# Two batches interleaved: batch 0 begins with six column tiles of the MLP, and three changeovers between batches 0 and 1 instead of five

## The chip, the cores and the metric

The kernel runs on one core of one Trainium2 chip. The metric is the device time of one execution in microseconds (us), the median of several runs. A profile of one execution shows what each engine did: TensorE (PE, with its weight loads as PEld), VectorE (DVE), ScalarE (ACT), GpSimd (POOL), and the queue SP, which here only issues DMAs. All times inside the execution count from the first instruction.

## The reference

An attention between 512 tokens and 32 state rows, in both directions, for 8 batches of 8 heads, and behind it one MLP with squared ReLU over all 4,608 rows:

```python
B, H, S, Ns, D = (8, 8, 512, 32, 64)
scores = scale * x @ state.T ;  a = softmax(scores);   xread = a @ state
scores2 = scale * state @ x.T;  a2 = softmax(scores2); sread = a2 @ x
rows = concatenate([xread, sread])            # 512 + 32 rows for each batch, 8 heads x 64 = 512 columns
out = relu(rows @ w_in) ** 2 @ w_out          # 512 -> 2048 -> 512
```

The weights `w_in` and `w_out` arrive as 64-bit floats and are brought to 32 bits on the chip.

## The kernel before

**Arithmetic.** Each large matmul is done as three: every float is split into a rounded high part and a rest (`split`: a cast on ACT at L97, a subtraction on DVE or POOL at L98), and hi x hi, lo x hi and hi x lo are summed.

**State first.** The kernel never forms `xread`. For the tokens it multiplies the state with `w_in` once (`z_part`: `L192` for the first six pieces, `L204` for the others), writes the result `zd` to DRAM and reads back what a batch needs (`z_fetch`, `L230`). The first matmul of the MLP is then attention weights times z.

**A unit.** The MLP works on one batch (512 tokens) and one column tile of 128 of the 2,048 hidden columns at a time, 16 column tiles (`NFC`) for each batch. I call this a unit, and number the units from 1 as they are worked through. In `mlp`, `up` issues 6 matmuls (L394) into `ph`; ACT takes the ReLU (L396); the square is ACT's for the first ten units (L398) and DVE's from then on (L400); ACT casts to `g_hi` (L97), and DVE closes the unit with `g_lo` (L98). `down` then issues 12 matmuls (L420) into four accumulators `po`, one for each 128 tokens. `down` runs two units behind `up`.

**Parts and changeovers.** `BOTH` (L67) cuts the column tiles of batches 0 and 1 into parts that alternate: an entry (b, c) means that batch b goes on to column tile c. At the end of a part `rows` empties the four accumulators into `sums[b]`: in a batch's first part by two copies on DVE (L441) and two on ACT (L439), in later parts by four adds on DVE (L601). Behind (0, NFC) and (1, NFC) the batches 2 to 7 follow whole, and at the end the same MLP runs once for the 256 state rows.

**Weights.** Each column tile needs two conversions on DVE. For `w_in`: a load into `w_raw` (L159), an absolute value on ACT (L107), then four DVE steps (L108, L109, L113, L117) that give `wf`; `wf` goes to DRAM (`wd`) and, from the seventh piece on, is split into `w` (L97, L98). For `w_out`: a load into `wo_raw` (L446), the same five steps to `wof`, and a split into `wo_hi` and `wo_lo` (POOL at L98). The raw words share `RAW` = 4 buffers, `wf` and `wof` have two each.

**Attention.** For batches 0 and 1 the scores run as plain matmuls (`pst`, L301) behind a scaling of the state (L248), then two softmaxes (L306 to L342). From batch 2 on they run as split matmuls (L291, with `sp_hl` from L251 and L252). The attention's weights `a_hi`, `a_lo` must be there before the batch's first unit. Two loads of x for each batch (L267) and two for the way back (L273) go through SP.

**What sets the order.** The class `Ahead` holds two lists of steps, `weights` and `reads` (the attention and its way back), each group with a due time in slots (two a unit): for weights twice the unit at which a column tile is first used (`at`, L466), for the attention of batch b twice the unit at which b begins, less one (`begins`, L567). `aux`, called twice a unit, issues as many steps as the due times ask for. Behind that, a scheduler moves instructions on each engine by its own estimate of their times; the engines then run them in the order printed in the section on the change.

Of the kernel before, what the change touches and what calls it, by code (L numbers as in the profile page):

```python
# [18 lines left out]
def memory_attention_then_relu2_ffn(  # L19
# [33 lines left out]
    NFC = DF // P  # L53
# [10 lines left out]
    XRAW = 2  # L64
    PLAIN_Z = 6
    PLAIN_X = 2
    BOTH = ((0, 2), (1, 6), (0, 10), (1, 10), (0, NFC), (1, NFC))  # L67
    LATE = 3

    def pool_early(early):  # L70
# [385 lines left out]
    parts, upto = [], [0] * B  # L456
    for b, c in BOTH + tuple((b, NFC) for b in range(2, B)):
        parts.append((b, range(upto[b], c)))
# [217 lines left out]
```

## Time and profile before

| what | value |
|---|---|
| median of 3 runs | 734.75 us (734.13 to 735.08) |
| the profiled execution | 734.07 us, of which 732.2 us are its span |
| granted TensorE clock, mean | 0.963 |
| HBM read and written | 60.03 MB and 29.88 MB |
| the chain that ended last | PE 74%, DMA 11%, DVE 8%, ACT 3% |

The page gives busy times and shares for each engine; a busy share is a mean over stages that have different limits. Its second part cuts the span into 40 slices of 18.3 us, with the busy share of each engine in tenths. A view by stretches gives busy time in any stretch, the granted TensorE clock (1.00 is full speed) and the share of time that the 16 DMA engines were busy. The timeline has one row for each instruction or run of like instructions: start, duration, engine, line, output and inputs, and in brackets the idle time ahead of it and what ended it. Durations overlap, since an engine begins an instruction before the one ahead has ended; the distance of two starts is what an instruction costs in a row of like ones.

### The profile page before, as it was taken

How to read it: one execution, taken by the hardware profiler on the slowest of the kernel's cores; microseconds unless marked ns; L12 is line 12 of the kernel's file. 1: busy time of each engine (PE TensorE's matmuls, PEld its weight loads, DVE VectorE, ACT ScalarE, POOL GpSimd, SP SyncE). 2: the span in 40 equal slices, each digit the busy share in tenths (PEclk: the TensorE clock that was granted, in tenths of full speed). 3: DMA queues.
4: the chain of work that ended last, by engine and by line, in shares of the span. 5: the costliest groups of instructions: out<-in, count | busy, mean ns of one | idle time of the engine just before them, and what ended most of it. 6: DMA issues, size and time to landing. Idle time of an engine off the chain costs nothing.

```text
span 732.2 us, 9312 instructions
## 1 busy us (share of the span) xinstructions
PE 679.1 (93%) x3152; PEld 554.3 (76%) x3152; DVE 476.6 (65%) x797; ACT 392.7 (54%) x711; POOL 197.6 (27%) x181
## 2 busy tenths in 40 slices
PE   4865898889999899999999999999999999999994
PEld 1434677768888788888888878878888888888893
DVE  5889798798956944356954694797755445443541
ACT  2656477566766664357654554656554345332441
POOL 2334121146662540025402322343152022000000
PEclk9677799999999999999999999999999999999998
DMA  9757877684464641143433211422141012100410
GB/s 265 252 175 249 243 244 235 201 221 133 133 213 129 195 127 59 47 140 119 136 108 116 86 59 58 143 87 86 60 144 58 31 33 82 42 1 9 135 59 30
DMA packets 72435, 90.52 MB, mean 124 GB/s; under 512 B 3780, under 2 KB 55748, under 8 KB 72388
## 3 DMA queue, kind: packets, MB, share of 16 engines
q1 hardware_dynamic: 54980, 73.15, 32.2%
q10 hardware_dynamic: 17408, 16.78, 6.8%
q8 instruction: 25, 0.41, 0.3%
q14 instruction: 22, 0.18, 0.1%
HBM read 60.03 MB, written 29.88 MB: 123 GB/s over the span
## 4 chain that ended last, share of the span: by engine, by line
PE 74%; DMA 11%; DVE 8%; ACT 3%; issue 2%; SPq 0%; POOL 0%; ACTq 0%; DVEq 0%
PE po L420 43%; PE ph L394 23%; DMA wo_raw<-w_out 3%; DMA z_raw<-zd 3%; PE pr L357 2%; PE pz L204 2%; DMA xn_raw<-xn 2%; DMA st_f<-stT 1%; PE pq L291 1%; DMA zd<-z_stage 1%; DVE sp_hl L252 1%; PE pz L192 1%; DVE wof L113 1%; DVE wof L117 1%; PE pt L345 1%
## 5 line engine op out<-in xcount | busy, mean ns | idle before, releaser
L420 PE MATMUL po<-wo_hi,g_hi 128*128 128x512 f32 x544 | 219.1, 405 | 15.5 <-ACT g_hi L97 12.1
L420 PE MATMUL po<-wo_lo,g_hi 128*128 128x512 f32 x544 | 216.4, 399 | 0.0
L400 DVE TENSOR_TENSOR ph<-ph,r 128x512 f32<-128x512 f32 (+1 forms) x134 | 89.0, 664 | 152.0 <-ACT r L396 151.9
L396 ACT ACTIVATE r<-ph 128x512 f32<-128x512 f32 (+1 forms) x144 | 82.6, 574 | 168.1 <-PE ph L394 167.4
L420 PE MATMUL po<-wo_hi,g_lo 128*128 128x512 f32 x544 | 152.4, 392 | 0.4
L420 PEld LDWEIGHTS po<-wo_hi,g_hi 128*128 128x128 f32 x544 | 103.9, 191 | 39.9 <-ACT g_hi L97 14.7
L420 PEld LDWEIGHTS po<-wo_lo,g_hi 128*128 128x128 f32 x544 | 104.9, 193 | 20.3 <-issue 0.7
L420 PEld LDWEIGHTS po<-wo_hi,g_lo 128*128 128x128 f32 x544 | 101.3, 189 | 22.0 <-DVE g_lo L98 1.6
L98 DVE TENSOR_TENSOR g_lo<-ph,g_hi 128x512 fp32r<-128x512 f32 (+1 forms) x144 | 94.5, 656 | 34.2 <-ACT g_hi L97 24.6
L97 ACT CAST g_hi<-ph 128x512 fp32r<-128x512 f32 (+1 forms) x144 | 81.1, 563 | 43.0 <-DVE ph L400 37.8
L394 PE MATMUL ph<-a_hi,z_hi 128*128 128x512 f32 x256 | 81.4, 399 | 0.6 <-DVE g_lo L98 0.6
L394 PE MATMUL ph<-a_hi,z_lo 128*128 128x512 f32 x256 | 79.7, 393 | 0.0
L394 PE MATMUL ph<-a_lo,z_hi 128*128 128x512 f32 x256 | 79.3, 391 | 0.0
L98 POOL TENSOR_TENSOR xn_hl<-xn_raw,xn_hl 128x1024 fp32r<-128x1024 f32 x16 | 39.2, 2449 | 147.9 <-ACT xn_hl L97 79.6
L183 POOL TENSOR_TENSOR w<-wf,w 64x512 fp32r<-64x512 f32 x32 | 43.5, 1360 | 59.6 <-ACT w L182 52.5
L394 PEld LDWEIGHTS ph<-a_hi,z_lo 128*128 128x128 f32 x256 | 48.4, 189 | 11.0 <-DVE z_lo L98 0.3
L394 PEld LDWEIGHTS ph<-a_hi,z_hi 128*128 128x128 f32 x256 | 47.8, 193 | 11.5 <-DVE g_lo L98 1.3
L394 PEld LDWEIGHTS ph<-a_lo,z_hi 128*128 128x128 f32 x256 | 48.2, 189 | 10.3
L98 DVE TENSOR_TENSOR z_lo<-z_raw,z_hi 128x512 fp32r<-128x512 f32 x64 | 50.2, 784 | 4.3 <-ACT z_hi L97 4.3
L97 ACT CAST z_hi<-z_raw 128x512 fp32r<-128x512 f32 x64 | 39.4, 615 | 12.3 <-DMA z_raw<-zd 11.9
L98 POOL TENSOR_TENSOR xt_hl<-xt_raw,xt_hl 128x1024 fp32r<-128x1024 f32 x12 | 29.3, 2438 | 58.5 <-ACT xt_hl L97 36.0
L98 POOL TENSOR_TENSOR wo_lo<-wof,wo_hi 128x512 fp32r<-128x512 f32 x16 | 22.5, 1407 | 79.4 <-ACT wo_hi L97 79.4
(98 smaller groups left out, 854.4 us busy)
## 6 DMA issues: line engine op xcount, KB each, us to landing
zd<-z_stage ACTq DMA_DIRECT2D x64, 256.0 KB
z_raw<-zd SPq DMA_DIRECT2D x63, 256.0 KB
xt_raw<-xT SPq DMA_DIRECT2D x16, 512.0 KB
w_raw<-w_in SPq DMA_DIRECT2D x16, 512.0 KB
wo_raw<-w_out SPq DMA_DIRECT2D x16, 512.0 KB
xn_raw<-xn SPq DMA_DIRECT2D x16, 512.0 KB
out<-sum SPq DMA_DIRECT2D x32, 256.0 KB
wd<-wf SPq DMA_DIRECT2D x16, 256.0 KB
```

The source lines that it names most:

```text
L97: nc.scalar.copy(out=hi, in_=src)
L98: eng_lo.tensor_sub(out=lo, in0=src, in1=hi.bitcast(F32))
L113: nc.vector.scalar_tensor_tensor(out=bits, in0=high, scalar=-0x40000000, in1=bits, op0=ALU.bitwise_and, op1=ALU.bitwise_or,)
L117: nc.vector.scalar_tensor_tensor(out=bits, in0=low, scalar=29, in1=bits, op0=ALU.logical_shift_right, op1=ALU.bitwise_or,)
L183: nc.gpsimd.tensor_sub(out=w[other], in0=wf[own], in1=w[own].bitcast(F32))
L192: nc.tensor.matmul(pz[:, q, :], lhsT=st["raw"][own, h, :], rhs=box["wf"][own, q, :], start=True, stop=True,)
L204: nc.tensor.matmul(pz[:, q, :], lhsT=a[:, h, :], rhs=w, start=j == 0, stop=j == len(todo) - 1,)
L357: nc.tensor.matmul(pr[:, q].rearrange("p i c -> p (i c)"), lhsT=my["e"][:, t, q].rearrange("p i n -> p (i n)"), rhs=my["xn"][:, t, q].rear ...
L394: nc.tensor.matmul(ph, lhsT=w, rhs=v, start=i == 0, stop=i == len(todo) - 1)
L396: nc.scalar.activation(r, ph, AF.Relu)
L400: nc.vector.tensor_mul(out=ph, in0=ph, in1=r)
L420: nc.tensor.matmul(po[t], lhsT=g, rhs=w, start=i == 0 and j == 0, stop=i == last and j == 2)
```

## The change

```diff
-    BOTH = ((0, 2), (1, 6), (0, 10), (1, 10), (0, NFC), (1, NFC))
+    BOTH = ((0, 6), (1, 10), (0, NFC), (1, NFC))
```

The 32 units of batches 0 and 1 run in this order, as ranges of column tiles:

| | units 1-2 | 3-6 | 7-8 | 9-16 | 17-20 | 21-26 | 27-32 |
|---|---|---|---|---|---|---|---|
| before | batch 0: 0-1 | batch 1: 0-3 | batch 1: 4-5 | batch 0: 2-9 | batch 1: 6-9 | batch 0: 10-15 | batch 1: 10-15 |
| now | batch 0: 0-1 | batch 0: 2-5 | batch 1: 0-1 | batch 1: 2-9 | batch 0: 6-9 | batch 0: 10-15 | batch 1: 10-15 |

Column tiles 2 to 5 are first used at units 3 to 6 instead of 5 to 8, tiles 6 to 15 at the same units as before. Batch 1 begins at unit 7 instead of unit 3, so its attention falls due four units later. Changeovers between the two batches stand ahead of units 7, 17 and 27 instead of 3, 9, 17, 21 and 27. Eight of the sixteen adds of L601 fall away: each batch has two parts instead of three. Nothing else is removed or added; the numbers of matmuls, loads and conversions stay the same.

How the instructions move shows in the printed order of each engine. Counted on DVE, the instructions ahead of and with a unit's closing `g_lo`:

| closing step of unit | 3 | 5 | 7 | 9 | 13 | 15 | 17 | 24 |
|---|---|---|---|---|---|---|---|---|
| before | 108 | 126 | 143 | 160 | 193 | 212 | 229 | 282 |
| now | 97 | 132 | 160 | 175 | 206 | 219 | 226 | 273 |

At the three places below, the rows are DVE's (`wf`: w_in's conversion, `wof`: w_out's, `w_1`: the low part of a split piece of w_in, `g_lo`: a unit's closing step). The first place is the way from the sixth to the seventh closing step. Before, the whole of it:

```order
L98 TENSOR_TENSOR g_lo<-ph,g_hi 128x512
L113 SCALAR_TENSOR_TENSOR wof<-wo_raw,wof 128x512
L117 SCALAR_TENSOR_TENSOR wf<-w_raw,wf 128x512
L117 SCALAR_TENSOR_TENSOR wof<-wo_raw,wof 128x512
L108 TENSOR_SCALAR wof<-wof 128x512
L109 TENSOR_SCALAR wof<-wof 128x512
L98 TENSOR_TENSOR w_1_741<-wf,w_0_740 128x512
L113 SCALAR_TENSOR_TENSOR wof<-wo_raw,wof 128x512
L98 TENSOR_TENSOR g_lo<-ph,g_hi 128x512
```

Now, its last eleven of 27 rows:

```order
L109 TENSOR_SCALAR wf<-wf 128x512
L108 TENSOR_SCALAR wof<-wof 128x512
L113 SCALAR_TENSOR_TENSOR wf<-w_raw,wf 128x512
L98 TENSOR_TENSOR w_1_871<-wf,w_0_870 128x512
L109 TENSOR_SCALAR wof<-wof 128x512
L117 SCALAR_TENSOR_TENSOR wf<-w_raw,wf 128x512
L98 TENSOR_TENSOR z_lo<-z_raw,z_hi 128x512
L113 SCALAR_TENSOR_TENSOR wof<-wo_raw,wof 128x512
L117 SCALAR_TENSOR_TENSOR wof<-wo_raw,wof 128x512
L98 TENSOR_TENSOR w_1_990<-wf,w_0_989 128x512
L98 TENSOR_TENSOR g_lo<-ph,g_hi 128x512
```

Seven instructions stood between the two closing steps; now 25 do, the last transposition of batch 1's attention and two copies of accumulators among the rows not shown. On PE the products of state and w_in that run as L204 stand further ahead in return: 72 of them, instead of 35, come before the seventh unit's first L420.

The second place is the end of the weights' conversions. Before, it lies behind the sixteenth closing step (the first row here), and the adds are those of the changeover ahead of unit 17:

```order
L98 TENSOR_TENSOR g_lo<-ph,g_hi 128x512
L108 TENSOR_SCALAR wof<-wof 128x512
L109 TENSOR_SCALAR wof<-wof 128x512
L113 SCALAR_TENSOR_TENSOR wof<-wo_raw,wof 128x512
L117 SCALAR_TENSOR_TENSOR wof<-wo_raw,wof 128x512
L400 TENSOR_TENSOR ph<-ph,r 128x512
L601 TENSOR_TENSOR sum<-sum,po_950 128x512
L601 TENSOR_TENSOR sum<-sum,po_951 128x512
L601 TENSOR_TENSOR sum<-sum,po_952 128x512
L98 TENSOR_TENSOR g_lo<-ph,g_hi 128x512
```

Now it lies ahead of the fifteenth closing step (the fifth row here; the eighth is the sixteenth):

```order
L109 TENSOR_SCALAR wof<-wof 128x512
L113 SCALAR_TENSOR_TENSOR wof<-wo_raw,wof 128x512
L117 SCALAR_TENSOR_TENSOR wof<-wo_raw,wof 128x512
L400 TENSOR_TENSOR ph<-ph,r 128x512
L98 TENSOR_TENSOR g_lo<-ph,g_hi 128x512
L400 TENSOR_TENSOR ph<-ph,r 128x512
L98 TENSOR_TENSOR z_lo<-z_raw,z_hi 128x512
L98 TENSOR_TENSOR g_lo<-ph,g_hi 128x512
L400 TENSOR_TENSOR ph<-ph,r 128x512
L441 COPY sum<-po_874 128x512
L441 COPY sum<-po_876 128x512
```

The last conversion has moved from the changeover to a place two units ahead of it, and two copies stand where three adds stood.

The third place is the changeover from batch 1 to batch 2, ahead of unit 33. Before (`st`, `sp_hl`, `q` and `at` belong to the attention of later batches):

```order
L297 TENSOR_TENSOR st<-pq,st_low 64x512
L251 TENSOR_SCALAR sp_hl<-sp_raw 64x4x32
L329 STREAM_TRANSPOSE at<-q_2322 128x512
L251 TENSOR_SCALAR sp_hl<-sp_raw 64x4x32
L400 TENSOR_TENSOR ph<-ph,r 128x512
L252 SCALAR_TENSOR_TENSOR sp_hl<-sp_raw,sp_hl 64x4x32
L297 TENSOR_TENSOR st<-pq,st_low 64x512
L252 SCALAR_TENSOR_TENSOR sp_hl<-sp_raw,sp_hl 64x4x32
L601 TENSOR_TENSOR sum<-sum,po_1760 128x512
L601 TENSOR_TENSOR sum<-sum,po_1761 128x512
L601 TENSOR_TENSOR sum<-sum,po_1762 128x512
```

Now:

```order
L297 TENSOR_TENSOR st<-pq,st_low 64x512
L400 TENSOR_TENSOR ph<-ph,r 128x512
L601 TENSOR_TENSOR sum<-sum,po_1744 128x512
L601 TENSOR_TENSOR sum<-sum,po_1745 128x512
L98 TENSOR_TENSOR g_lo<-ph,g_hi 128x512
L601 TENSOR_TENSOR sum<-sum,po_1746 128x512
L601 TENSOR_TENSOR sum<-sum,po_1747 128x512
L400 TENSOR_TENSOR ph<-ph,r 128x512
```

The writing of `sp_hl` and the transposition have moved behind the adds.

On SP, the two loads of batch 2's x move from behind the sixth and seventh load of w_in to behind the ninth and eleventh.

## The prediction

> **What bounds the kernel now.** I read the page first: which engine is full, and when.
>
> ```profile
> PE 679.1 (93%) x3152; PEld 554.3 (76%) x3152; DVE 476.6 (65%) x797; ACT 392.7 (54%) x711; POOL 197.6 (27%) x181
> PE   4865898889999899999999999999999999999994
> DVE  5889798798956944356954694797755445443541
> DMA  9757877684464641143433211422141012100410
> ```
>
> TensorE (PE) is the bound, but not from the start: its slices are full only from about the tenth on (18.3 us each). Before that VectorE (DVE) and the DMA engines have high digits. So the change, which rearranges the first 32 units, can only give or take time where PE still waits. The table by stretches sizes that (PE, PEld, DVE, ACT, POOL busy; then the granted clock, the DMA share, GB/s):
>
> ```profile
> 20.00:47.00 27.00, 19.75 (x47) 10.79 (x47) 21.70 (x47) 16.14 (x36) 8.19 (x7) 0.69 0.70 226
> 47.00:100.00 53.00, 40.97 (x165) 31.36 (x164) 46.36 (x77) 31.19 (x57) 16.38 (x12) 0.81 0.72 223
> 100.00:150.00 50.00, 44.84 (x214) 36.47 (x213) 41.86 (x70) 31.41 (x59) 9.47 (x7) 0.97 0.74 234
> 150.00:170.00 20.00, 17.12 (x75) 13.63 (x74) 18.20 (x24) 13.99 (x26) 11.56 (x8) 0.91 0.68 191
> 170.00:240.00 70.00, 70.00 (x338) 58.45 (x338) 53.38 (x93) 47.80 (x85) 36.01 (x31) 1.00 0.47 148
> 240.00:250.00 10.00, 8.14 (x41) 6.24 (x40) 9.91 (x15) 7.05 (x14) 7.39 (x5) 1.00 0.49 153
> ```
>
> From 170 to 240 us PE works 70.00 of 70 us: nothing can be won there. Time is lost in the first 170 us and once more at 240 to 250. In each lossy stretch DVE is at 80 to 99%, so DVE's queue, which runs in program order, is what to count. A unit (one column tile of one batch) is closed on DVE by the step that writes g_lo; the timeline has the first, the seventh and the fifteenth of these at:
>
> ```profile
> 46.98 0.62 DVE L98 TENSOR_TENSOR g_lo<-ph,g_hi 128x512 fp32r<-128x512 f32 x1
> 100.02 0.68 DVE L98 TENSOR_TENSOR g_lo<-ph,g_hi 128x512 fp32r<-128x512 f32 x1
> 150.61 0.68 DVE L98 TENSOR_TENSOR g_lo<-ph,g_hi 128x512 fp32r<-128x512 f32 x1
> ```
>
> **The change part by part.** PE's work is the same; only its waits and its slow-clock time differ. I follow four places and count, from the order of the instructions, what DVE has to do ahead of a closing step. Prices are the groups by line:
>
> ```profile
> L108 DVE TENSOR_SCALAR wf<-wf 128x512 f32<-128x512 f32 x16 | 8.0, 500 | 9.4 <-ACT wf L107 9.4
> L109 DVE TENSOR_SCALAR wf<-wf 128x512 int32<-128x512 int32 x16 | 7.7, 484 | 0.2
> L113 DVE SCALAR_TENSOR_TENSOR wf<-w_raw,wf 128x512 int32<-128x512 int32 x16 | 15.2, 949 | 0.1
> L117 DVE SCALAR_TENSOR_TENSOR wf<-w_raw,wf 128x512 int32<-128x512 int32 x16 | 11.9, 746 | 0.0
> L108 DVE TENSOR_SCALAR wof<-wof 128x512 f32<-128x512 f32 x16 | 9.0, 560 | 7.7 <-ACT wof L107 7.7
> L109 DVE TENSOR_SCALAR wof<-wof 128x512 int32<-128x512 int32 x16 | 8.6, 540 | 0.2
> L113 DVE SCALAR_TENSOR_TENSOR wof<-wo_raw,wof 128x512 int32<-128x512 int32 x16 | 13.3, 834 | 0.1
> L117 DVE SCALAR_TENSOR_TENSOR wof<-wo_raw,wof 128x512 int32<-128x512 int32 x16 | 14.1, 882 | 0.1
> L98 DVE TENSOR_TENSOR w<-wf,w 128x512 fp32r<-128x512 f32 x10 | 8.6, 859 | 0.2
> L98 DVE TENSOR_TENSOR z_lo<-z_raw,z_hi 128x512 fp32r<-128x512 f32 x64 | 50.2, 784 | 4.3 <-ACT z_hi L97 4.3
> ```
>
> A, up to the seventh unit (batch 1's first one now). Ahead of its closing step stand 160 DVE instructions instead of 143. More are two conversions of w_in (0.500 + 0.484 + 0.949 + 0.746 = 2.68 each, 5.4), one of w_out with a second L117 (0.560 + 0.540 + 0.834 + 2 x 0.882 = 3.7), three splits of w (2.6) and one z_lo (0.8): 12.4 us. From 47 to 100 us DVE is idle for 53 - 46.36 = 6.6 us; if all that fills up, the closing step comes 12.4 - 6.6 = 5.8 us late, if none does, 12.4. I take 8.4, nearer the lower end, since the third closing step has 11 instructions fewer ahead of it than before (batch 1's attention no longer stands there), so this stretch starts earlier. Against that, PE has by then issued 72 instead of 35 of the products of state and w_in that run as 128x256 matmuls, one each 0.12 us:
>
> ```profile
> 159.36 0.28 PE L204 MATMUL pz<-w,stz_lo 128*128 128x256 f32 x1
> 159.48 0.40 PE L204 MATMUL pz<-w,stz_hi 128*128 128x256 f32 x2
> ```
>
> 37 x 0.12 = 4.4 us of PE's work done in advance. A = +8.4 - 4.4 = **+4.0 us** (1.4 to 8.0).
>
> B, from the seventh to the fifteenth unit. At the fifteenth 219 instructions stand against 212: two w_out conversions and one split more (5.6 + 0.9), two copies of 0.68 fewer: +5.1 us. So DVE has 12.4 - 5.1 = 7.3 us less to do in this stretch, of 41.86. PE loses 50 - 44.84 = 5.2 us to idleness here and 0.03 x 50 = 1.5 to the clock, together 6.7; the gain lies between 0 (if the loads of the weights set the pace, DMA share 0.74) and 6.7. With DVE clearly below PE's load but the loads unchanged I take half: **-3.3 us**.
>
> C, units 16 to 18. Here a changeover meets the last w_out conversions:
>
> ```profile
> 156.59 0.41 DVE L108 TENSOR_SCALAR wof<-wof 128x512 f32<-128x512 f32 x1
> 157.04 1.41 DVE L109 TENSOR_SCALAR wof<-wof 128x512 int32<-128x512 int32 x1
> 158.49 1.67 DVE L113 SCALAR_TENSOR_TENSOR wof<-wo_raw,wof 128x512 int32<-128x512 int32 x1
> 160.19 1.65 DVE L117 SCALAR_TENSOR_TENSOR wof<-wo_raw,wof 128x512 int32<-128x512 int32 x1
> 161.77 0.68 DVE L400 TENSOR_TENSOR ph<-ph,r 128x512 f32<-128x512 f32 x1
> 163.18 0.77 PE L420 MATMUL po<-wo_hi,g_hi 128*128 128x512 f32 x1 [2.58 <-ACT g_hi L97]
> 163.75 0.63 PE L420 MATMUL po<-wo_lo,g_hi 128*128 128x512 f32 x1
> 164.17 0.63 PE L420 MATMUL po<-wo_hi,g_hi 128*128 128x512 f32 x1
> 168.21 0.39 PE L420 MATMUL po<-wo_hi,g_hi 128*128 128x512 f32 x1
> 168.44 0.40 PE L420 MATMUL po<-wo_lo,g_hi 128*128 128x512 f32 x1
> ```
>
> The square of unit 17 (L400) stands behind four conversion steps; PE waits 2.58 us for the cast of that square, and then starts a matmul every 0.42 us (163.75, 164.17) until it is back at 0.23 (168.21, 168.44). The stretch loses 2.88 us idle and 0.09 x 20 = 1.8 to the clock: 4.7. In the change the conversions end ahead of the fifteenth closing step; what stands ahead of the seventeenth is two copies, and three adds are gone (229 instructions against 226). The changeover itself stays. Gain 0 to 4.7; I take **-3.5 us**, near the upper end, as the blocking rows are gone.
>
> [...]
>
> D, unit 33, where batch 2 begins:
>
> ```profile
> 239.89 2.52 DVE L252 SCALAR_TENSOR_TENSOR sp_hl<-sp_raw,sp_hl 64x128 fp32r<-64x128 f32 x1
> 244.56 0.47 PE L420 MATMUL po<-wo_hi,g_hi 128*128 128x512 f32 x1 [0.64 <-DVE sum L601]
> 247.45 0.50 PE L420 MATMUL po<-wo_hi,g_hi 128*128 128x512 f32 x1 [0.59 <-DVE sum L601]
> ```
>
> The adds that free the accumulators are held up by steps of the attention of the batches ahead, L252 above all. In the new order all but one of these steps stand behind the four adds. Gain 0 to 1.86 (10 - 8.14); I take **-1.5**.
>
> Costed at nothing: eight adds fewer at the changeovers. Four are counted in C's rows; the others fall where PE has no gap. On SP's queue the two loads of batch 2's x (512 KB each) move behind later weight loads; with a DMA share of 0.72 they fit into what is free, and if they did not, 1 MB at 223 GB/s would add 4.5 us, inside A's span. POOL's part of batch 1's attention moves along; POOL is busy 16.38 of 53 us there.
>
> Sum: +4.0 - 3.3 - 3.5 - 1.5 = -4.3. The profiled execution took 734.07 (span 732.2 and 1.9 around it), so 729.8; it lies 0.7 under the median of 734.75, on which the forecast is **730.5**.
>
> **The rivals.** *Unit 7 starves and nothing is made up.* Between the sixth and the seventh closing step DVE now has 25 instructions instead of 7, conversions for units far ahead among them, whose raw words must have landed. If the step comes the full 12.4 late (A +8.0) and the loads keep B at 0, C and D give +3.0: 737.8. It is slower than before as soon as A exceeds the 5.0 of C and D, that is from a seventh closing step at 100.0 + 4.4 + 5.0 = 109.4 us with B at 0. For it: DVE is at 87% there, and the loads have to come earlier too. Against: the DMA engines are 28% idle there. 0.22.
>
> *The loads decide anyway.* If the last weight words land when they do now, A and B cancel, C's wait only moves, and about half of D is left: -0.8, 734.0. For it: a DMA share of 0.72 to 0.74 for 100 us. Against: DVE at 18.20 of 20 in C, not the loads, holds the square back. 0.17.
>
> *All goes well.* A 1.4, B -5.5, C -4.7, D -1.9: -10.7, 724.1. 0.11. That the scheduler undoes the change is excluded: the new order has six units of batch 0 in a row.
>
> **How the numbers follow.** The forecast has 0.50. The bounds add up to -11.9 and +8.0 (722.9 to 742.8); both ends need every term at its end, so I leave out the outer few us on either side: 725.5 to 738.5. A measurement of this kernel can tell about 0.2%, 1.5 us. Faster by more: 0.50 + 0.11 = 0.61; within: 0.17; slower: 0.22.
>
> **What would show it.** A: the seventh closing step at 106 to 112 us, with a wait of PE of 3 us or more for g_hi before it. B: less than 5 us of idle PE between that and unit 15, DVE below 80%. C: no conversion step on DVE behind the fifteenth closing step, no half-rate matmuls around unit 17. D: no wait for the adds at batch 2's begin. The forecast is wrong if the seventh step comes after 112, or if the last w_out conversion still ends near 162 us.

## The result, and the profile after

| | median, us | runs | ratio to before, 95% interval |
|---|---|---|---|
| before, same chip | 734.44 | 733.62 to 735.08 (4) | |
| changed kernel | 726.25 | 723.62 to 726.73 (4) | 0.9882, 0.9856 to 0.9908 |
| again (e4) | 727.59 | 726.00 to 727.85 (4) | 0.9895, 0.9873 to 0.9917 |
| again (e19) | 725.85 | 724.36 to 726.75 (6) | 0.9897, 0.9870 to 0.9923 |

The change makes the kernel faster by 8.2, 6.5 and 7.5 us against the kernel before on the chip of each comparison (734.44, 734.11, 733.39). The forecast was 4.3 us of gain: the direction is right, the size is a little over half of what came.

The page of the changed kernel first, the busy times and then PE's slices:

```profile
PE 670.0 (93%) x3152; PEld 551.7 (76%) x3152; DVE 470.8 (65%) x789; ACT 393.5 (55%) x711; POOL 200.5 (28%) x181
PE   4577779999999999999999999999999999999994
```

PE is at 90% or more from the seventh slice (108 us) to the last but one, where before it was so from the tenth (165 us); the six slices ahead still are not. Three stretches of the view, with the same bounds as before (PE, PEld, DVE, ACT, POOL busy; clock, DMA share, GB/s):

```profile
47.00:100.00 53.00, 39.13 (x169) 29.42 (x167) 49.66 (x85) 33.86 (x64) 17.58 (x12) 0.90 0.74 249
100.00:150.00 50.00, 45.73 (x216) 37.94 (x217) 45.48 (x71) 34.50 (x66) 18.21 (x11) 0.97 0.80 244
150.00:170.00 20.00, 20.00 (x92) 16.61 (x91) 15.69 (x29) 15.04 (x26) 11.87 (x7) 1.00 0.34 109
```

From 150 to 170 us PE now has 20.00 of 20 us at clock 1.00, where it had 17.12 at 0.91. Between 100 and 150 us the change is small in this view (45.73 against 44.84), because the cut no longer falls on the same units. So from here on I count by units. On DVE, the seventh closing step, the last step of the last w_out conversion, and the fifteenth closing step:

```profile
105.55 0.68 DVE L98 TENSOR_TENSOR g_lo<-ph,g_hi 128x512 fp32r<-128x512 f32 x1
...
144.07 0.69 DVE L117 SCALAR_TENSOR_TENSOR wof<-wo_raw,wof 128x512 int32<-128x512 int32 x1
...
147.19 0.69 DVE L98 TENSOR_TENSOR g_lo<-ph,g_hi 128x512 fp32r<-128x512 f32 x1 [1.82 <-ACT g_hi L97]
```

**Lost time by units.** For each kernel I sum PE's work up to the end of a unit's 12 down matmuls (full-rate distances of two starts, medians over the trace: in before 0.227 us for the 512-column L420, 0.12 us for the 256-column L204, and so on) and subtract it from the time of that end. What is left is PE's loss up to there, waits and half-rate matmuls together, and a kernel with more work done ahead isn't blamed for it. All kernels of this study, in us, at the ends of units:

| | 8 | 12 | 16 | 20 | 32 | 34 | median of runs |
|---|---|---|---|---|---|---|---|
| before | 42.8 | 47.0 | 50.8 | 55.2 | 54.8 | 57.7 | 733.2 to 734.4 |
| changed kernel | 43.5 | 45.3 | 47.5 | 47.1 | 47.5 | 47.5 | 726.25 |
| e4, the same | 47.7 | 47.6 | 49.9 | 49.7 | 49.4 | 49.5 | 727.59 |
| e19, the same | 47.5 | 47.6 | 49.8 | 49.6 | 49.5 | 49.5 | 725.85 |
| e1 | 42.5 | 43.4 | 50.2 | 53.1 | 52.7 | 52.3 | 732.62 |
| e2 | 47.3 | 47.8 | 52.2 | 55.3 | 54.8 | 57.6 | 733.37 |
| e3 | 51.9 | 51.5 | 51.9 | 54.6 | 54.0 | 56.7 | 732.25 |
| e5 | 45.3 | 46.6 | 48.7 | 48.2 | 53.7 | 54.7 | 732.42 |
| e6 | 44.9 | 46.9 | 50.1 | 54.5 | 54.9 | 54.7 | 730.33 |
| e7 | 45.0 | 46.9 | 51.0 | 51.3 | 50.7 | 50.7 | 726.25 |
| e8 | 44.9 | 52.2 | 54.2 | 54.2 | 54.5 | 54.5 | 728.03 |
| e9 | 44.6 | 49.2 | 52.7 | 55.6 | 56.4 | 59.3 | 733.88 |
| e10 | 41.5 | 45.5 | 49.1 | 52.1 | 52.2 | 52.2 | 731.77 |
| e12 | 50.8 | 51.0 | 52.6 | 54.8 | 54.5 | 54.1 | 730.13 |
| e13 | 45.8 | 51.1 | 52.8 | 52.6 | 52.0 | 52.0 | 729.46 |
| e14 | 44.1 | 51.1 | 55.1 | 59.4 | 59.0 | 59.0 | 735.67 |
| e15 | 43.7 | 47.5 | 50.6 | 56.4 | 63.2 | 63.3 | 740.90 |
| e16 | 40.3 | 51.2 | 51.0 | 50.8 | 50.9 | 50.4 | 727.92 |
| e17 | 46.2 | 48.1 | 50.6 | 51.3 | 51.2 | 50.8 | 728.52 |
| e18 | 47.7 | 50.5 | 51.7 | 51.7 | 51.8 | 51.9 | 727.65 |

One profile stands for each row, so a difference of 2 us that arises before the end of unit 1 says nothing: the first profile of the changed kernel, 723.62 us, has lost 22.8 us at the end of unit 1, its repeats e4 and e19 24.5 and 25.1. I read the terms from the repeats. Steps below zero, down to -0.6 us (e3, e7 and e13 from unit 20 to 32), show how closely a step can be trusted; the sum up to unit 8 is less certain, since the matmuls of the first units (L192, L301) have no steady distance (in before most lie between 0.05 and 0.59 us and between 0.43 and 1.02 us), and other prices for them shift it by about 1 us from kernel to kernel.

In every kernel the loss comes in a few steps of 2 to 9 us with flat stretches between. The rows behind the steps of before, and what stands there now:

*Units 7 and 8.* The changed kernel loses more here. PE, and what ACT does while PE waits:

```profile
101.58 0.58 PE L204 MATMUL pz<-w,stz_lo 128*128 128x256 f32 x1 [3.28 <-ACT z_stage L216]
98.93 1.08 ACT L396 ACTIVATE r<-ph 128x512 f32<-128x512 f32 x2
...
100.41 0.63 ACT L97 CAST wo_hi<-wof 128x512 fp32r<-128x512 f32 x1
100.93 0.60 ACT L216 COPY z_stage<-pz 128x512 f32<-128x512 f32 x1
```

PE has nothing but z products left, and for these the copy z_stage has to empty an accumulator (`pz`); on ACT it stands behind the ReLUs of two units, a cast of z (99.90 us) and the cast of a w_out tile. The wait is 3.28 us.

*Unit 9.* Before, ACT and PE:

```profile
112.61 0.66 ACT L107 ACTIVATE wof<-wo_raw 128x512 f32<-128x512 f32 x1 [2.07 <-DMA wo_raw<-w_out]
...
113.18 0.57 ACT L97 CAST g_hi<-ph 128x512 fp32r<-128x512 f32 x1
113.80 0.50 PE L420 MATMUL po<-wo_hi,g_hi 128*128 128x512 f32 x1 [2.03 <-ACT g_hi L97]
```

The absolute value of a w_out tile waits 2.07 us for its load, the cast g_hi stands behind it, and PE waits 2.03 us for that cast. In the changed kernel the same wait of ACT is even longer, but hardly reaches PE:

```profile
114.16 0.66 ACT L107 ACTIVATE wof<-wo_raw 128x512 f32<-128x512 f32 x1 [2.81 <-DMA wo_raw<-w_out]
...
114.72 0.57 ACT L97 CAST g_hi<-ph 128x512 fp32r<-128x512 f32 x1
115.35 0.50 PE L420 MATMUL po<-wo_hi,g_hi 128*128 128x512 f32 x1 [0.48 <-ACT g_hi L97]
```

2.81 us on ACT become 0.48 us on PE. Before, PE's wait was also followed by matmuls at half rate: the granted clock was 0.50 from 115.17 to 118.58 us. A changeover stood here, and ahead of the wait PE had only one unit's ups and 12 z products to run; now there are downs of the unit before among them (109.41 to 113.51).

*Unit 33.* The adds that free the accumulators when batch 2 begins, on DVE, and PE's first matmul behind its last down of the old batch:

```profile
227.32 1.28 DVE L601 TENSOR_TENSOR sum<-sum,po 128x512 f32<-128x512 f32 x2
...
229.11 1.27 DVE L601 TENSOR_TENSOR sum<-sum,po 128x512 f32<-128x512 f32 x2
228.60 0.39 PE L420 MATMUL po<-wo_hi,g_lo 128*128 128x512 f32 x1
228.83 0.62 PE L394 MATMUL ph<-a_hi,z_hi 128*128 128x512 f32 x2
```

PE goes on without a gap. Before, a step L252 of 2.52 us stood ahead of the adds, and beside it ran, on POOL:

```profile
239.87 2.40 POOL L98 TENSOR_TENSOR xn_hl<-xn_raw,xn_hl 128x1024 fp32r<-128x1024 f32 x1 [7.33 <-ACT xn_hl L97]
```

### The profile page after: what moved, and what is told of

The parts are those of the page before. It is cut to its first block, busy times and chain, and to the rows that moved or that the text cites. A ratio compares the mean times of both kernels' runs of the same rounds, so it can differ in the third digit from the quotient of the medians.

```text
span 721.4 us, 9309 instructions
## 1 busy us (share of the span) xinstructions
PE 670.0 (93%) x3152; PEld 551.7 (76%) x3152; DVE 470.8 (65%) x789; ACT 393.5 (55%) x711; POOL 200.5 (28%) x181
## 4 chain that ended last, share of the span: by engine, by line
PE 72%; DVE 17%; DMA 4%; ACT 3%; issue 3%; SPq 0%; POOL 0%; DVEq 0%; ACTq 0%; POOLq 0%
PE po L420 43%; PE ph L394 23%; PE pr L357 2%; DMA wo_raw<-w_out 2%; PE pz L204 2%; DVE wf L113 2%; DMA z_raw<-zd 1%; DVE sp_hl L252 1%; DVE z_lo L98 1%; DVE g_lo L98 1%; DVE wof L113 1%; PE pq L291 1%; PE pt L345 1%; DVE wf L117 1%; DVE wf L108 1%
## 5 line engine op out<-in xcount | busy, mean ns | idle before, releaser
L420 PE MATMUL po<-wo_hi,g_hi 128*128 128x512 f32 x544 | 217.4, 401 | 3.0 <-ACT g_hi L97 2.9
L420 PE MATMUL po<-wo_lo,g_hi 128*128 128x512 f32 x544 | 213.1, 393 | 0.0
L420 PE MATMUL po<-wo_hi,g_lo 128*128 128x512 f32 x544 | 151.3, 390 | 2.4 <-DVE g_lo L98 2.4
L420 PEld LDWEIGHTS po<-wo_hi,g_hi 128*128 128x128 f32 x544 | 103.3, 190 | 26.3 <-ACT g_hi L97 4.9
L420 PEld LDWEIGHTS po<-wo_hi,g_lo 128*128 128x128 f32 x544 | 101.0, 188 | 23.3 <-DVE g_lo L98 3.2
L420 PEld LDWEIGHTS po<-wo_lo,g_hi 128*128 128x128 f32 x544 | 103.5, 190 | 19.7 <-issue 0.2
L394 PEld LDWEIGHTS ph<-a_hi,z_lo 128*128 128x128 f32 x256 | 48.1, 188 | 10.4
L98 DVE TENSOR_TENSOR z_lo<-z_raw,z_hi 128x512 fp32r<-128x512 f32 x64 | 46.9, 733 | 2.5 <-ACT z_hi L97 2.5
L98 POOL TENSOR_TENSOR wo_lo<-wof,wo_hi 128x512 fp32r<-128x512 f32 x16 | 25.9, 1620 | 67.1 <-ACT wo_hi L97 67.1
```

The source lines that it names most:

```text
L98: eng_lo.tensor_sub(out=lo, in0=src, in1=hi.bitcast(F32))
L394: nc.tensor.matmul(ph, lhsT=w, rhs=v, start=i == 0, stop=i == len(todo) - 1)
L420: nc.tensor.matmul(po[t], lhsT=g, rhs=w, start=i == 0 and j == 0, stop=i == last and j == 2)
```

## The experiments

Theory and rivals changed on the way. The runs are told in the order of the questions; all are compared with the kernel before on the same chip.

### Is it the start, or the later changeovers?

e1 keeps the old start and the number of adds, e2 has the new start and the old number of changeovers:

```diff
 e1: BOTH = ((0, 2), (1, 6), (0, 6), (1, 10), (0, NFC), (1, NFC))
 e2: BOTH = ((0, 6), (1, 6), (0, 10), (1, 10), (0, NFC), (1, NFC))
```

> Units 1 to 12 as before (0-1 of batch 0, 0-5 of batch 1, 2-5 of batch 0), then 6-9 of batch 1, 6-15 of batch 0, 10-15 of batch 1: five changeovers and sixteen adds as before, but none ahead of unit 21. Theory 'front' (the gain comes from six column tiles of batch 0 ahead of batch 1's attention, through the conversions that end two units earlier; terms A, B, C): here the conversions end ahead of the 18th closing step, so A, B and C are not gained, only D (about 2 us): 732 to 733.5, seventh closing step near 100, conversions to about 162. Theory 'changeovers' (the gain is that of two changeovers and eight adds): as many of both as before, so no gain, 733.5 to 735. If the start decides nothing: 727 to 729.

Measured 732.62 us, ratio 0.9974 (0.9952 to 0.9996).

> Six column tiles of batch 0 first as in the change, then the later parts as before in kind (0-5 of batch 1, 6-9 of batch 0, 6-9 of batch 1, then 10-15 of both): again five changeovers and sixteen adds. Theory 'front': the conversions end ahead of the 14th closing step, so A, B and C are gained, D is not (batch 2's begin has the order of before): 727.5 to 729.5. Theory 'changeovers': no gain, 733.5 to 735. PE lost up to unit 18 about 47 us by the first, 54 to 55 by the second.

Measured 733.37 us, ratio 0.9992 (0.9973 to 1.0012). The new start alone brings nothing: at the end of unit 12 e2 stands where the changed kernel stands (47.8 against 47.6), at the end of unit 34 it has lost all that the change gains (57.6 against 49.5), 4.4 us by unit 16, 3.1 by unit 20, and 2.8 at unit 33. "Front" fell with e2. "Changeovers" had 733.5 to 735 us for both runs; e2 lies next to that, e1 in the range of "front", so neither theory fits both. In e1 the step of before at unit 9 is missing and another one stands at its new changeover, unit 13. There on ACT and PE:

```profile
133.21 0.66 ACT L107 ACTIVATE wof<-wo_raw 128x512 f32<-128x512 f32 x1 [6.58 <-DMA wo_raw<-w_out]
135.92 0.58 PE L204 MATMUL pz<-w,stz_lo 128*128 128x256 f32 x1 [3.61 <-ACT z_stage L216]
```

e3 sets batch 1's attention to begin four units earlier again, as before:

```diff
-            reads.add(steps, 2 * begins[b] - 1, 2 * ends[b - 2] if b > 1 else 0)
+            reads.add(steps, 2 * (begins[b] if b > 1 else 2) - 1, 2 * ends[b - 2] if b > 1 else 0)
```

> The change, but batch 1's attention keeps the due time that it had before (slot 3 instead of 11). If A's good result comes from keeping that attention out of the way of the first weights, the third closing step is later than in the change (67.9 us there) by the 5 us or so that attention costs on DVE and the kernel ends 2 to 4 us later than the change (728 to 730). If only the order of the units matters, it ends within 1 us of the change (725.5 to 727).

Measured 732.25 us, ratio 0.9975 (0.9948 to 1.0002). It costs about 5 us of the gain (732.25 against 727.59), more than the 2 to 4 that I expected, and not in the way that I expected: the third closing step comes at 62.95 us, earlier than the change's 67.86, and the loss follows it. 51.9 us are lost at the end of unit 8 in place of 47.6, the longest wait behind that step being one of 5.88 us, up to 80.68 us, for a cast of z on ACT. Unit 33 loses 2.7 us again. That batch 1's attention moves along with its first unit is part of the change's gain.

e4, the changed kernel unaltered:

> The changed kernel once more, as a reference on the same chip and for a second profile. 725.5 to 727. The first profile of it, with 723.6, was the fastest of four runs; if that is chance in the first 30 us, whose order is the same in all kernels here, the first L394 starts later here than 29 us, and the seventh closing step comes at 106 to 108 instead of 105.6.

Measured 727.59 us, 0.6 above the expected range, ratio 0.9895 (0.9873 to 0.9917); the seventh closing step at 107.46 us.

### Do changeovers cost as such, and is it their adds?

e5 has one changeover fewer and four adds fewer than the changed kernel; e8 begins with four tiles:

```diff
 e5: BOTH = ((0, 6), (1, NFC), (0, NFC))
 e8: BOTH = ((0, 4), (1, 10), (0, NFC), (1, NFC))
```

> Two parts for batch 0, one whole for batch 1: changeovers ahead of units 7 and 23 only, four adds in place of eight. Theory 'phase' (a changeover costs PE 3 to 7 us while DVE still converts weights, to about 147 us, and nothing later): the same as the changed kernel, 726 to 728 us. Theory 'adds' (every changeover with its adds costs alike, (734.4 - 726.3) / 2 = 4 us each): 722 to 724 us.

Measured 732.42 us, ratio 0.9976 (0.9956 to 0.9996). Both theories fell: fewer changeovers and fewer adds, and most of the gain is gone. Up to unit 20 e5 is as good as the changed kernel; then it loses 5.5 us. On DVE, POOL and PE:

```profile
172.52 0.28 DVE L252 SCALAR_TENSOR_TENSOR sp_hl<-sp_raw,sp_hl 64x128 fp32r<-64x128 f32 x1
...
173.43 2.09 DVE L252 SCALAR_TENSOR_TENSOR sp_hl<-sp_raw,sp_hl 64x128 fp32r<-64x128 f32 x1
172.98 2.40 POOL L98 TENSOR_TENSOR xn_hl<-xn_raw,xn_hl 128x1024 fp32r<-128x1024 f32 x1 [0.82 <-ACT xn_hl L97]
179.52 0.66 PE L420 MATMUL po<-wo_hi,g_hi 128*128 128x512 f32 x1 [2.24 <-ACT g_hi L97]
179.97 0.63 PE L420 MATMUL po<-wo_lo,g_hi 128*128 128x512 f32 x1
180.40 0.63 PE L420 MATMUL po<-wo_hi,g_hi 128*128 128x512 f32 x1
```

It is the hold of before's unit 33 in another place. L252 takes 0.28 us alone and 2.09 us beside POOL's split, nine steps of attention stand ahead of a unit's square (178.06 us), PE waits 2.24 us for the cast behind them and then runs at half rate (179.97 to 180.40 us: 0.43 us for one matmul).

> Batch 0 begins with four column tiles: changeovers ahead of units 5, 15 and 27, with the same eight adds as the changed kernel. 'phase': the changeover at 15 falls on the last conversions and costs 3 to 4 us, 729 to 732 us, with waits of PE between 145 and 155 us. 'adds': the same as the changed kernel, 726 to 728 us.

Measured 728.03 us, ratio 0.9930 (0.9904 to 0.9956), between the two ranges. The loss at unit 15 is 2 us, less than expected; the large step is at unit 10, where there is no changeover at all. On ACT and PE:

```profile
121.45 0.66 ACT L107 ACTIVATE wf<-w_raw 128x512 f32<-128x512 f32 x1 [7.46 <-DMA w_raw<-w_in]
125.23 0.58 PE L204 MATMUL pz<-w,stz_lo 128*128 128x256 f32 x1 [5.40 <-ACT z_stage L216]
```

ACT waited 7.46 us for a load, and the copy z_stage, which stands behind that wait on ACT, held PE for 5.40 us. e6 and e7 are e2 without some of its emptyings:

```diff
 e6, in rows(), ahead of everything else:
+            if b == 1 and fcs[0] == 0:
+                return
-            if fcs[0] == 0:
+            if fcs[0] == (6 if b == 1 else 0):
 e7:
-            else:
+            elif fcs[-1] == NFC - 1:
                 nc.vector.tensor_add(out=sums[b][:, t, :], in0=sums[b][:, t, :], in1=po)
```

> e2 (changeovers ahead of 7, 13, 17, 21, 27) without emptying the accumulators ahead of unit 13: two copies on DVE and two on ACT are left out, and with them the column tiles 0 to 5 of batch 1 in the output. If the emptying is what the changeover at 13 costs, the 4.6 us lost between the ends of units 12 and 15 in e2 become about 1, and the time is 729 to 731 us. If it is the order of the ups and downs around the changeover, 732.5 to 734 us, the loss still 3 to 5 us.

Measured 730.33 us, ratio 0.9957 (0.9938 to 0.9976). The time lies in the range of "emptying", but not for its reason: units 13 to 15 still lose 3.4 us (46.9 to 50.3), and 4.4 come up between the ends of units 16 and 20, where PE waits 1.82 us up to 170.89 us and then runs at half rate. What e6 gains over e2 is unit 33, which loses nothing here and 2.8 us there.

> e2 without the adds of the parts that are neither a batch's first nor its last (emptyings ahead of units 17 and 21, eight adds; the column tiles 6 to 9 of batches 0 and 1 are missing from the output). 'adds': as the changed kernel, 725 to 728 us. 'phase': only what e2 loses around units 17 and 18 comes back, 2 to 3 us: 730 to 732 us, with the loss at units 13 to 15 and that at unit 33 unchanged.

Measured 726.25 us, ratio 0.9895 (0.9862 to 0.9929): as "adds" had it. The lost time says why, and it isn't the price of the adds: units 13 to 15 lose 4.6 us as in e2, units 17 to 20 lose 0.3 in place of 3.1, and unit 33 loses nothing. With the adds gone, the scheduler ordered DVE's steps around them anew. To separate adds from order I took the adds from the kernel before.

### Unit 17 and unit 33 by themselves

e10 is e7's edit made on the kernel before; e9 takes from DVE the two squares that stand behind conversion steps there:

```diff
 e10:
-            else:
+            elif fcs[-1] == NFC - 1:
                 nc.vector.tensor_add(out=sums[b][:, t, :], in0=sums[b][:, t, :], in1=po)
 e9:
-            if units[0] < 10:
+            if units[0] < 10 or units[0] in (16, 17):
                 nc.scalar.activation(ph, r, AF.Square)
```

> The kernel before without the eight adds of the middle parts (the emptyings ahead of units 17 and 21; the column tiles 2 to 9 of batch 0 and 6 to 9 of batch 1 are missing from the output). DVE's order up to unit 17 keeps its conversion steps, and ahead of unit 33 it becomes that of the changed kernel. 'DVE's queue': the loss at unit 17 stays at 3.5 to 4.6 us, that at unit 33 (2 to 2.6 us) goes: 731.5 to 732.5 us. 'adds': as the changed kernel, 725 to 728 us.

Measured 731.77 us, ratio 0.9973 (0.9955 to 0.9991), as "DVE's queue" had it. At unit 33 nothing is lost (52.2 at units 32 and 34), with the order of the changed kernel there. At unit 17 still 3.2 us are (49.1 to 52.3; I had named 3.5 to 4.6), though the three adds behind the square are gone. On DVE and PE:

```profile
156.35 0.42 DVE L108 TENSOR_SCALAR wof<-wof 128x512 f32<-128x512 f32 x1
156.80 1.40 DVE L109 TENSOR_SCALAR wof<-wof 128x512 int32<-128x512 int32 x1
158.24 1.66 DVE L113 SCALAR_TENSOR_TENSOR wof<-wo_raw,wof 128x512 int32<-128x512 int32 x1
159.93 1.65 DVE L117 SCALAR_TENSOR_TENSOR wof<-wo_raw,wof 128x512 int32<-128x512 int32 x1
161.50 0.69 DVE L400 TENSOR_TENSOR ph<-ph,r 128x512 f32<-128x512 f32 x1
162.86 0.50 PE L420 MATMUL po<-wo_hi,g_hi 128*128 128x512 f32 x1 [2.48 <-ACT g_hi L97]
163.19 0.39 PE L420 MATMUL po<-wo_lo,g_hi 128*128 128x512 f32 x1
163.43 0.39 PE L420 MATMUL po<-wo_hi,g_hi 128*128 128x512 f32 x1
```

The four conversion steps are those of the prediction, row for row, and PE waits 2.48 us in place of 2.58. What is missing is the half rate: 163.19 to 163.43 is 0.24 us. That is the 1.4 us by which the loss is smaller; the last section sets the two waits side by side. That it depends on when the wait falls, not on the adds, is my estimate from there.

> The kernel before, with the squares of units 17 and 18 on ACT in place of DVE; all parts, adds and conversions stay. 'DVE's queue' (the square of unit 17 stands behind four conversion steps on DVE, and that wait with its half-rate matmuls is the whole loss of 4.4 us there): the loss between the ends of units 16 and 17 falls from 4.6 to under 1.5 us, 730 to 731.5 us. 'adds' (the eight extra adds cost): unchanged, 733.5 to 735 us.

Measured 733.88 us, ratio 1.000 (0.9974 to 1.0026): no gain, against the theory's 730 to 731.5, and 3.1 us lost at unit 17 against its 1.5. On DVE and PE:

```profile
163.52 1.65 DVE L117 SCALAR_TENSOR_TENSOR wof<-wo_raw,wof 128x512 int32<-128x512 int32 x1
165.10 2.47 DVE L601 TENSOR_TENSOR sum<-sum,po 128x512 f32<-128x512 f32 x4
166.36 0.50 PE L420 MATMUL po<-wo_hi,g_hi 128*128 128x512 f32 x1 [2.43 <-DVE sum L601]
```

With the square out of the way, the adds stand behind the same four steps, and PE waits 2.43 us for them. So it is the conversion steps that hold PE up, through whatever stands behind them. Moving one victim away leaves another; what the change does is to have the conversions done before unit 15.

### POOL beside DVE

In several of these rows a step of DVE is stretched. Before, on POOL, beside the conversion steps of the prediction (157.04 to 161.84 us):

```profile
156.80 1.37 POOL L98 TENSOR_TENSOR wo_lo<-wof,wo_hi 128x512 fp32r<-128x512 f32 x1 [4.02 <-ACT wo_hi L97]
158.25 3.04 POOL L183 TENSOR_TENSOR w<-wf,w 64x512 fp32r<-64x512 f32 x2
```

L117 takes 1.65 us there, and 0.69 us at 144.07 us in the changed kernel; L109 takes 1.41 us and ends 0.28 us after the operation of POOL that began ahead of it, and the next two steps run beside POOL's next two. L252 took 0.28 us alone in e5 and 2.52 us beside POOL's split in before. Over the whole trace of before, the 25 steps L117 with no operation of POOL beside them took 0.67 to 0.69 us, the seven with one 0.64 to 1.80; the five L252 without one took 0.28 or 0.29 us, the seven with one 0.28 to 2.52. So a step beside POOL is stretched at times, and which one is, and why, these rows don't show. The stretching is about as long as what PE waits. The four conversion steps take 5.25 us in before (156.59 to 161.84); at what such steps take unstretched in the changed kernel (0.41, 0.41, 0.68 and 0.68 us) they would take 2.2, which is 3.0 less, against a wait of 2.58. L252 takes 2.2 us more than alone at unit 33, where 2.9 are lost, and 1.8 more in e5, where PE waits 2.24. So without POOL's operations beside them most of these waits would be gone: that is an estimate from these rows, and no run here tests it at these places. e12 puts the low part of w_out's split on DVE in the changed kernel:

```diff
-        split(wo[k][0][:, i, :], wo[k][1][:, i, :], wf, nc.gpsimd)
+        split(wo[k][0][:, i, :], wo[k][1][:, i, :], wf, nc.vector)
```

> The changed kernel with the low part of w_out's split on DVE in place of POOL. If the steps of DVE that took 1.4 to 1.7 us in place of 0.41 to 0.68 were held up by an operation of POOL that ran beside them, the mean of L109, L113 and L117 of wof falls by 0.1 us or more each, from 0.54, 0.83 and 0.88 us. DVE gets 16 x 0.68 = 10.9 us more to do ahead of unit 15; if the shorter steps do not make up for it, the time is 728 to 733 us, if they do, 724 to 727 us.

Measured 730.13 us, ratio 0.9933 (0.9910 to 0.9955): slower than the changed kernel. Two groups of the changed kernel, then of e12:

```profile
L113 DVE SCALAR_TENSOR_TENSOR wf<-w_raw,wf 128x512 int32<-128x512 int32 x16 | 15.6, 977 | 0.0
L113 DVE SCALAR_TENSOR_TENSOR wof<-wo_raw,wof 128x512 int32<-128x512 int32 x16 | 12.0, 751 | 0.1
```

```profile
L113 DVE SCALAR_TENSOR_TENSOR wf<-w_raw,wf 128x512 int32<-128x512 int32 x16 | 12.5, 784 | 0.0
L113 DVE SCALAR_TENSOR_TENSOR wof<-wo_raw,wof 128x512 int32<-128x512 int32 x16 | 12.9, 804 | 0.1
```

The expectation had L109, L113 and L117 of w_out fall by 0.1 us each from the means of the kernel before, and it failed: they come to 0.48, 0.80 and 0.83 us, 0.03 to 0.06 less. Against the changed kernel L109 falls (576 to 478 ns), L113 and L117 rise (751 to 804 and 743 to 828 ns); all four steps of w_in get shorter (L113 977 to 784 ns). All eight groups of L108 to L117 together fall from 89.6 to 79.4 us, and the 16 low parts add 12.3: DVE gains nothing, and PE's wait ahead of unit 7 grows to 5.11 us.

### Which part of units 7 to 16?

e13 and e17 move changeovers of the changed kernel, e14, e15 and e16 have the old start:

```diff
 e13: BOTH = ((0, 8), (1, 12), (0, NFC), (1, NFC))
 e17: BOTH = ((0, 6), (1, 12), (0, NFC), (1, NFC))
 e14: BOTH = ((0, 2), (1, 10), (0, NFC), (1, NFC))
 e15: BOTH = ((0, 2), (1, 6), (0, NFC), (1, NFC))
 e16: BOTH = ((0, 2), (1, 8), (0, NFC), (1, NFC))
```

> Batch 0 begins with eight column tiles: changeovers ahead of units 9, 21 and 29. The wait ahead of the changed kernel's unit 7 (3.3 to 3.7 us for z_stage) should stay, since DVE's steps up to there hardly differ (155 against 160 at the seventh closing step). 'DVE's queue': no conversion steps stand ahead of the squares near units 17 and 21, so the time is that of the changed kernel, 725.5 to 728.5 us. 'changeovers cost while weights convert': the one at 9 costs 3 us or more, 729 to 731 us.

Measured 729.46 us, ratio 0.9944 (0.9924 to 0.9964), in the range of "changeovers". The wait ahead of unit 7 stays without a changeover there (3.93 us for z_stage at 103.95 us), so the first term of the prediction doesn't need the changeover. A second wait of that kind stands at unit 9, where this kernel changes over:

```profile
121.11 0.38 PE L204 MATMUL pz<-w,stz_lo 128*128 128x256 f32 x1 [3.25 <-ACT z_stage L216]
```

> New start, changeovers ahead of units 7, 19 and 29, eight adds. Both theories: the same as the changed kernel, 725.5 to 728.5 us, with a loss of about 50 us at the end of unit 15 and nothing after it; a bundle of attention steps between two closing steps, as in e5 at unit 21, would add 2 to 4 us.

Measured 728.52 us, ratio 0.9933 (0.9917 to 0.9948): at the upper end of what was expected (725.5 to 728.5), with 50.6 us lost at the end of unit 16 and 0.2 behind it by unit 34.

> Old start (two tiles of batch 0), then ten of batch 1: changeovers ahead of units 3, 13 and 27, eight adds. 'changeovers': no loss between the ends of units 7 and 12 (under 1.5 us; before 5.4), 3 to 6 us at units 13 to 15, none at 17: 728 to 731 us. 'advance of the conversions': the loss between units 7 and 12 stays above 3 us: 731 to 734 us.

> Old start and batch 1 up to tile 6 as before, then batch 0 to its end and batch 1 to its end: changeovers ahead of units 3, 9 and 23. DVE's order up to unit 13 is that of the kernel before, so the loss there should be too (47 to 49 us at the end of unit 13); what follows has no changeover until 23: under 2 us between units 13 and 20. 'changeovers': 726.5 to 729.5 us. 'advance of the conversions': the squares of units 15 to 17 still stand behind conversion steps, 3 to 4 us lost there, 730 to 732 us.

> Old start, then eight tiles of batch 1: changeovers ahead of units 3, 11 and 25. 'changeovers': a loss of 3 us or more at units 11 to 13 and none at 9 and 17: 728 to 731 us. 'advance of the conversions': a loss of 3 us or more at unit 9 or 10 already: 731 to 734 us.

Measured 735.67 us (ratio 1.0030, 1.0008 to 1.0051), 740.90 us (1.0094, 1.0067 to 1.0122) and 727.92 us (0.9927, 0.9910 to 0.9945). "Changeovers" fell: e14 and e16 have no changeover at unit 9 and lose 7.0 and 10.9 us between units 8 and 12, more than the kernel before. These two use column tiles from the seventh on for the first time at unit 9; before and now that is at unit 13. In e16, on ACT and PE:

```profile
108.22 0.62 ACT L97 CAST z_hi<-z_raw 128x512 fp32r<-128x512 f32 x1 [3.42 <-DMA z_raw<-zd]
...
115.85 0.62 ACT L97 CAST z_hi<-z_raw 128x512 fp32r<-128x512 f32 x1 [0.81 <-DMA z_raw<-zd]
117.01 0.79 PE L420 MATMUL po<-wo_hi,g_hi 128*128 128x512 f32 x1 [5.58 <-ACT g_hi L97]
```

The read of z has not landed (3.42 us, and 0.81 again), ACT holds the cast g_hi behind it, and PE waits 5.58 us. e15 follows before up to unit 13, as expected (47.5 us), and then uses all the tiles from the seventh on at units 13 to 22: it loses 8.9 us by unit 20 and 7.1 more at unit 23. "Advance of the conversions" is right on where the losses lie, but wrong on all three times: it had 731 to 734, 730 to 732 and 731 to 734 us. e14 and e15 lose more than it had, and e16 loses nothing more behind unit 11.

### Is what is left DVE's?

e18 is the changed kernel with the squares of units 11 to 16 on ACT:

```diff
-            if units[0] < 10:
+            if units[0] < 16:
```

> The changed kernel with the squares of units 11 to 16 on ACT in place of DVE, six steps of 0.7 us fewer on DVE. 'DVE's queue holds units 13 to 16': the 2.3 us lost between the ends of units 12 and 15 become under 1, and the time is 1 to 2 us under the changed kernel's in the same comparison. 'Something else holds them' (loads, or ACT, which then has the squares in its own queue): no difference beyond 0.5 us, or slower.

Measured 727.65 us, ratio 0.9917 (0.9888 to 0.9946), beside 725.85 us for the changed kernel in the same comparison:

> The changed kernel once more: 726 to 728 us, a loss of 45 to 48 us at the end of unit 12 and 47 to 50 at the end of unit 15, nothing at units 17 and 33.

The second alternative: units 12 to 15 lose 1.2 us in place of 2.5, but 2.1 come up at unit 11, where PE waits 1.81 us for g_hi on ACT. The intervals of the two ratios overlap. None of the orders tried is faster than the changed kernel; e7 is as fast and leaves work out.

## Why the prediction fell short, and what it had right

The direction was right, and the sum was about half of what came. The step that failed most is B: the prediction let late weight loads pass through to PE and so took half of that stretch's 6.7 us, 3.3; nearly all of the rest came too, 5.8 and 5.7 in the repeats. C and D were sized too small as well, by 1.1 and 1.3 us. By lost time, against before:

| term | forecast, us | measured, e4 and e19, us | first profile, us |
|---|---|---|---|
| A, up to the end of unit 8 | +4.0 (1.4 to 8.0) | +4.9, +4.7 | +0.7 |
| B, units 9 to 16 | -3.3 (-6.7 to 0) | -5.8, -5.7 | -4.0 |
| C, units 17 to 20 | -3.5 (-4.7 to 0) | -4.6, -4.6 | -4.8 |
| D, units 33 and 34 | -1.5 (-1.86 to 0) | -2.8, -2.9 | -2.9 |
| sum | -4.3 | -8.3, -8.5 | -11.0 |

(B is 42.8 to 50.8 before against 47.7 to 49.9 and 47.5 to 49.8, and so on. The profiled executions e4 and e19 took 726.0 and 726.75 us, 8.1 and 7.3 less than the 734.07 of before, the first one 723.62, 10.5 less.) In the first profile, which was ahead at the end of unit 1, A and B share the time otherwise: A and B together are -3.3 there, and -0.9 and -1.0 in the repeats, against +0.7 in the forecast. So B's miss is known to 1 or 2 us only; C's and D's are the same in all three.

**A** came in the size that was worked out: the seventh closing step at 105.55, 107.46 and 108.94 us in the three profiles, against 106 to 112. The wait ahead of it is there too, 3.28, 3.25 and 3.00 us, but for z_stage on ACT, not for g_hi. The prediction had DVE's steps hold that unit up; no run here shows that they are what makes ACT late, so it may be luck that the size came out. e13 shows that the wait doesn't need the changeover.

**B is the step that failed**, by 2.5 and 2.4 us in the repeats. The prediction took "half" of 6.7 us, because the loads might set the pace. The loads still come late for ACT, 2.81 us at 114.16, but that cost PE 0.48 us, where before 2.07 us cost it 2.03; I put that down to what PE has to run meanwhile. Units 7 to 12 now use only tiles that batch 0 has used already. All eleven kernels with six tiles first, the changed one and its repeats among them, lose between -0.4 and 2.8 us from the end of unit 8 to that of unit 12. Four with before's order up to unit 9 lose 3.8 to 4.6, and three that use new tiles there (e8, e14, e16) 7.3, 7.0 and 10.9; e13, whose new tiles reach to unit 8, as before's do, loses 5.3, nearly all of it at unit 9. So the tiles' first use goes with the losses in all of these. One speaks against a simple rule: e1 has before's order up to unit 9, with the changeover, and lost 0.9, where ACT waited 1.35 us for the load in place of 2.07. So how B divides into the changeover at unit 9, the tiles' first use and the chance of a load isn't settled, and its cause stays open to that extent. What I had named to show it was wrong as well: DVE was to fall below 80%, and by the stretch from the seventh to the fifteenth closing step it is at 90%, from 84% before. Its work there did fall, by 4.9 us (42.45 to 37.53; 7.3 were forecast), but the stretch itself fell from 50.59 to 41.64 us:

```profile
105.55:147.19 41.64, 38.97 (x188) 31.82 (x187) 37.53 (x60) 26.34 (x50) 13.81 (x10) 1.00 0.77 235
```

PE has 38.97 of 41.64 us at clock 1.00 all the same, under 5 us idle as forecast. A DVE that was busy for 37.53 of 41.64 us left PE 2.67 us idle here, of which one wait of 1.03 us (up to 142.56) was for a step of DVE.

**C** was right in its mechanism and 1.1 us short: nearly all of the 4.7 came, since both the wait and the half rate went. e10 and e9 show the mechanism from two sides. The half rate, 1.4 us of this by e10, is chance by my estimate: with nearly the same wait, 2.48 us against 2.58, e10 has none of it. The last w_out conversion now ends at 144.8 us, ahead of the fifteenth closing step. The three adds, which I counted along with the conversions, were not needed for it.

**D** was right in its mechanism and outside its bounds in size. e10 shows the mechanism alone, and so does e3: with the change's parts and adds it has before's order at unit 33 again, L252 of 2.52 us at 238.00 us ahead of the adds, and loses 2.7 us. The bound was PE's idle time in a window, 1.86 us, which is the sum of three waits there: 0.63 us for L297 at 243.18, of the same bundle on DVE, and 0.64 and 0.59 for the adds. But PE counts as busy also while a matmul waits for its accumulator: in before the six matmuls of L420 that start from 244.56 to 246.00 us stand 0.29 us apart on the mean in place of 0.23 (those at 244.56, 245.10 and 245.67 each follow the end of an add, at 244.41, 245.02 and 245.61), 0.3 us in all. And around each wait about 0.3 us more are lost than the gap shows: the L204 ahead counts as busy for 0.28 us, where its distance is 0.12, and the first matmul behind it takes longer (247.45 to 247.79, 0.34 us in place of 0.23). Idle time wasn't an upper bound.

Costing eight adds at nothing as work was right by e10; what they do to the scheduler's order, together with the time at which batch 1's attention falls due (e3), was D itself. Of the rivals, "all goes well" came close in B and C (5.5 and 4.7), had A too small (1.4) and D too (1.9); unit 7 did starve, but not by the 8.0 us of "nothing is made up"; and "the loads decide anyway" fell with B.

## What to carry to other kernels

Count what a stall costs in work not done, unit by unit; here the idle time of a window left out half-rate matmuls (1.4 us at unit 17) and matmuls that waited for an accumulator (0.3 us at unit 33). Here, where each engine works through its printed order, the loss comes as a few separate holds, and each is a bundle of unrelated steps ahead of the one that PE needs; taking away the victim only finds the next one (e9), and a rearrangement that has nothing against it on paper can put the same bundle in another place (e5, e15). Before halving a gain because a load may come late, look at what PE has to run while it is late: here 2.81 us of lateness cost it 0.48.

## What the runs showed of the hardware, not expected

Half-rate matmuls do not follow from the length of the last wait alone. They came behind waits of 1.82 us (e6), 2.03 us (before, unit 9), 2.24 us (e5) and 2.58 us (before, unit 17), and not behind 2.43 us (e9: starts at 166.70 and 166.94 us) and 2.48 us (e10). They go with the granted clock: in before it was 0.50 from 115.17 to 118.58 us and from 162.96 to 166.37 us, at the waits of units 9 and 17. Between 50 and 700 us the clock is 1.00 or 0.50 in the traces of before and of the changed kernel. The stretches at 0.50 that begin there start at 57.15, 70.80, 87.87, 115.17 and 162.96 us in before and last 6.83, 6.83, 3.41, 3.41 and 3.41 us; in the changed kernel they start at 60.25, 80.73 and 101.21 us and last 3.41, 6.83 and 3.41 us. Two neighbouring windows of 3.41 us around the wait at unit 17, of before, up to the start of its stretch at 0.50 and from there, and then of e10 (PE busy first; the clock is the third number from the right):

```profile
159.55:162.96 3.41, 1.05 (x9) 0.85 (x8) 3.38 (x4) 1.08 (x2) 1.99 (x3) 1.00 0.26 90
162.96:166.37 3.41, 3.19 (x8) 2.54 (x9) 3.41 (x7) 3.41 (x7) 2.13 (x2) 0.50 0.99 296
...
158.07:161.49 3.42, 2.31 (x16) 1.93 (x14) 3.35 (x3) 0.54 (x1) 2.88 (x2) 1.00 0.46 142
161.49:164.90 3.41, 2.04 (x9) 1.70 (x10) 2.59 (x5) 3.29 (x7) 1.29 (x1) 1.00 0.71 209
```

In before 2.36 us of the wait fall into one window, and the next one runs at 0.50. In e10 the wait is cut into 1.11 and 1.37 us, and the clock is 1.00 in both. In the traces of before and of the changed kernel, cut from the starts above in steps of 3.41 us between 50 and 700 us, each of the eight windows at 1.00 with 1.91 to 2.91 us of PE idle was followed by one at 0.50, and none with 1.51 us or less was. So two waits of nearly the same length cost 4.6 us (before, 2.58 us) and 3.2 us (e10, 2.48 us) at unit 17; that it is chance, by where a wait falls, which of the two it costs is my estimate from these windows.

A step of DVE beside one of POOL took nine times as long as alone: L252 0.28 us alone (e5), 2.52 us in before beside a split of 2.40 us on POOL that began 0.02 us earlier.
